# The first attention batch of a fused attention and MLP kernel: norms and Newton one slot sooner, its mix right behind the rank, landmark scaling on ACT, and 232 small unread products ahead of TensorE's queue

## The chip, the cores and the metric

The kernel runs on one core of a Trainium2 chip. The engines are named as the profile names them: PE (matrix products; PEld is its loading of weights), DVE (VectorE), ACT (ScalarE), POOL (GpSimd) and SP, whose queue issues most of the DMAs. The metric is the time of one execution on the device in microseconds; shorter is better.

## The reference

Three stages follow each other, in float32, for a batch of 8, with 576 tokens and a width of 512.

```python
# 1: Nystrom attention; 8 heads of 64, 32 landmarks (means over 18 tokens), scale 1/8
A, Bm, C = sm(q, k_lm), sm(q_lm, k_lm), sm(q_lm, k)
Z = Bm.T / (norm1(Bm) * norminf(Bm) + 1e-6)
for _ in range(6):
    Z = 2 * Z - Z @ Bm @ Z
x = A @ Z @ C @ v
# 2: a rank-32 mix over the tokens, then an MLP 512 -> 2048 -> 512
u = x + (x.T @ U @ V).T
x = u + relu(u @ w_ch1) @ w_ch2
# 3: a real 2-D Fourier mix, layer norm, a second MLP of the same size
u = x + real(fft2(x))
y = u + relu(layernorm(u) @ w_ch1) @ w_ch2
```

The MLP weights and U and V arrive as float64 words, and the kernel makes float32 of them on the chip.

## The kernel before

The MLPs are nearly all of the products. Each of their float32 products is made of three reduced ones (high by high, high by low, low by high), in chunks of 512 tokens, so that weights and activations have to be split into a high and a low part first: ACT copies the high part, DVE or POOL subtracts it.

The work runs in slots that are written out by hand. `Batch.steps` yields pairs of a slot number and a step for one batch of the attention, and the program runs them slot by slot; the order in which the steps are recorded is the order in which each engine takes its instructions, so an instruction that waits holds everything behind it on its engine. The steps of batch 0 begin at slot -21. From slot 0 the steps of a batch stand between pieces of the first MLP pass (`mlp.stream(0)`, whose products are L238 to L240 and L291 to L293). Batch 1 begins so early that its first steps lie among the last ones of batch 0. Ahead of the first MLP product PE thus has the whole of batch 0 and the first half of batch 1.

A batch goes as follows. `landmark` sums 18 tokens at a time on DVE (L726) and scales the sums into the tiles `kb` and `qb` (L728, on POOL), whose other places are zeroed once at the start. `kernel` multiplies `qb` and `kb` (L759, eight products, four column groups of 32 beside each other) and `kernel_norm` and `kernel_t` make Bm, its transpose and the sums behind its norms on DVE. `scores` is C (L823 and L828), with its maxima on DVE (L831) and its exponentials on ACT (L837 and L839). `norms` (L792), `residue` (L806) and six times `newton` (L969) make Z. `query` is A (L896, L903), `values` (L874) is C @ v, `mixed` (L951, L955) A @ U, `heads` (L984) and `rank` (L995) join them, and `mix` (L1011) writes two of the four blocks of u: ACT copies them out of PSUM (L1014), and they are split into the tiles `x` that the MLP reads (L50 and L51).

Two kinds of products fill slots: landmark sums of a later batch (`landmark_sums`, L738), and products of the identity matrix with itself that nobody reads (L1543). Beside this the weights of the first pass are converted on DVE, ACT and POOL (`convert`, L95 to L105, called by `direct`), from raw tiles that SP fetches (L87).

Of the kernel before, what the change touches and what calls it, by code (L numbers as in the profile page):

```python
# [9 lines left out]
F32 = mybir.dt.float32  # L10
# [12 lines left out]
LM, W = 32, 18  # L23
P = 128
# [11 lines left out]
def f32(ap):  # L36
    return ap.bitcast(F32)
# [3 lines left out]
def body(ctx: ExitStack, tc: tile.TileContext, qT, kT, vn, mU, mV, w11, w12, w21, w22,  # L41
         ident, bones, istack, tabs, out):
    nc = tc.nc
# [42 lines left out]
    def fetch_raw(raw, src):  # L86
        nc.sync.dma_start(raw, src.bitcast(U32))  # L87
# [82 lines left out]
    class Mlp:  # L170
# [17 lines left out]
        def fetch(self, nm, src):  # L188
            t = f32(self.weight(nm))
            if isinstance(src, tuple):  # L190
                for n, part in enumerate(src):
                    nc.sync.dma_start(t[:, :, 256 * n:256 * n + 256], part)
            else:
                nc.sync.dma_start(t, src)
# [461 lines left out]
    UB = 4  # L656

    def attention_constants(cp, t):
        t["ident"] = cp.tile([P, P], F32, name="ident_sb")
        nc.sync.dma_start(t["ident"], ident)  # L660
        t["U"] = cp.tile([P, 6, R], F32, name="U_sb")
        t["v"] = cp.tile([P, 5, DM], F32, name="v_")
        t["ETt"] = cp.tile([P, 2, P], F32, name="ETt")
        nc.gpsimd.memset(t["v"][64:P, 4, :], 0.0)
        nc.gpsimd.memset(t["ETt"][64:P], 0.0)
        for nm in ("kb", "qb"):
            t[nm] = cp.tile([P, 4, 64], F32, name=nm)
            nc.gpsimd.memset(t[nm], 0.0)
        for nm, src, n in (("bones", bones, P), ("istack", istack, R)):
            t[nm] = cp.tile([P, n], F32, name=nm + "_sb")  # L670
            nc.sync.dma_start(t[nm], src)
        t["at"] = cp.tile([P, 4, S], F32, name="at")
        t["W"] = cp.tile([P, 4, 64], F32, name="W")
# [22 lines left out]
    class Batch:  # L696
# [25 lines left out]
        def landmark(self, nm, g):  # L722

            src, dst = getattr(self, nm)[:, 2 * g:2 * g + 2, :], self.t[nm + "b"]
            s_ = self.pool.tile([P, 2, LM], F32, name="ls", bufs=2)
            nc.vector.tensor_reduce(s_, src.rearrange("p e (m w) -> p e m w", w=W), axis=AX.X, op=ALU.add)  # L726
            for j in range(2):
                nc.gpsimd.tensor_scalar_mul(dst[64 * j:64 * j + 64, 2 * g:2 * g + 2, 32 * (j ^ g):32 * (j ^ g) + 32],  # L728
                                            s_[64 * j:64 * j + 64], 1.0 / W if nm == "k" else 0.125 / W)

        def landmark_sums(self, nm, first, last):

# [55 lines left out]

        def norms(self):

            ps = self.bank("n" if self.b > 1 else "b")
            nc.tensor.matmul(ps[:, 0:P], self.t["bones"], self.dg.rearrange("p a b -> p (a b)"), start=True, stop=True)  # L792
            n = self.stat(4).rearrange("p (g k) -> p g k", k=2)
            nc.vector.tensor_reduce(n.rearrange("p g k -> p (g k)"), ps[:, 0:P].rearrange("p (a b) -> p a b", b=R),
                                    axis=AX.X, op=ALU.max)
            self.c = self.stat(2)
            nc.vector.tensor_tensor(self.c, n[:, :, 0], n[:, :, 1], op=ALU.mult)
            nc.vector.tensor_scalar_add(self.c, self.c, 1e-6)
            nc.vector.reciprocal(self.c, self.c)
# [221 lines left out]
        def steps(self, after):  # L1021

            H0, H1 = slice(0, 512), slice(512, 1152)
            a, b = (2, 1) if self.b > 1 else (0, 0)
            yield from ((2 * (nm == "q") + g - a, lambda nm=nm, g=g: self.landmark(nm, g)) for nm in "kq"
                        for g in (0, 1) if (self.b, nm) not in LANDMARKS)
            yield from ((5 - a, self.kernel), (6 - a, self.kernel_norm), (7 - a, self.kernel_t))
            if a:
                yield 6, self.norms
            yield 6, self.scores  # L1030
            if not a:
                yield 8, self.norms
            yield 9 - b, self.residue
            yield from ((10 - b + i, lambda i=i: self.newton(i)) for i in range(6))
            yield from ( (8, lambda: self.query(0)), (9, lambda: self.query(1)),
                        (9, lambda: self.query_exp(H0)), (9, self.scores_sum), (9, lambda: self.query(2)), (10, lambda: self.scores_t(0)),
                        (11, lambda: self.scores_t(1)), (11, self.scores_tail), (11, lambda: self.query_exp(H1)),
                        (11, lambda: self.query_norm(H0)), (12, self.values), (12, lambda: self.query_norm(H1)),
                        (13, lambda: self.query_t(0)), (13, self.query_tail), (14, lambda: self.query_t(1)),
                        (15, self.mixed), (16 - b, self.heads), (17 - b, self.rank))  # L1040
            if self.b:
                yield 13, lambda: self.mlp.get_tail(self.b)
                yield from ((15 + k // 2, lambda k=k: self.mlp.hand_tail(self.b, k)) for k in range(4))
            yield from ((19 + g, lambda g=g, n=n: self.mix(g, n)) for g in range(2) for n in range(2))
            if after:
                yield from ((r, lambda nm=nm: after.load(nm)) for r, nm in ((7, "k"), (10, "q"), (13, "v")))

# [269 lines left out]
    def pool(name, **k):  # L1317
        return tc.tile_pool(name=name, bufs=1, reuse_waits="tile", **k)
# [5 lines left out]
    def some(gen, n):  # L1324
        for _ in range(n):
            next(gen, 0)
# [156 lines left out]
    with pool("mm") as mp, pool("pm", space=PSUM) as pm:  # L1483
        mlp = Mlp(mp, pm, 3, passes)

        def direct():

            ws = [mlp.weight(nm) for nm in ("w1", "w2") for _ in range(HM)]
            raws = []
            seq = [*range(4), *range(HM, 2 * HM, 2), *range(4, HM), *range(HM + 1, 2 * HM, 2)]  # L1490

            def fetch():
                i = len(raws)
                if i < len(ws):
                    if i < EARLY:
                        raw = f32(mp.tile([P, 2, 512], F32R, name="g", bufs=HM)).rearrange(
                            "p a n -> p (a n)").bitcast(U32)
                    else:
                        raw = cv0.tile([P, 1024], U32, name="wraw", bufs=2)
                    fetch_raw(raw, srcs[0][seq[i]])  # L1500
                    raws.append(raw)

            for n in range(2):
                fetch()
                yield 1

            old = None
            for n, i in enumerate(seq):
                while len(raws) < min(max(n + 2, min(n + 3, EARLY)), len(ws)):
                    fetch()  # L1510
                new = convert(cv0, raws[n], ws[i], 2)
                for g in (new, old, old, new):
                    if g:
                        yield next(g)
                old = new
            yield from old

        EARLY = 8
        with pool("aa") as ap_, pool("ac") as ac, pool("cv0") as cv0, pool("pt", space=PSUM) as psb:
            t = {}  # L1520
            batches = [Batch(ap_, psb, t, b, mlp) for b in range(B)]
# [23 lines left out]
            with tc.manual_schedule():  # L1545
                for what in "kq":
                    batches[0].load(what)
                attention_constants(ac, t)
                small, large = attention_setup(t, ap_, cv0), direct()
                some(small, 1)  # L1550
                some(large, 1)
                batches[0].load("v")
                some(large, 1)
                convs = chained([small, large])
                for s in range(FIRST, 0):
                    slots.run(s)
                    if s - FIRST in (6, *range(10, 20)):
                        filler(s)
                    some(convs, 0 if s < FIRST + 4 else 1 + s % 2)
                later, gen = staging(cv0, 1, 2), mlp.stream(0)  # L1560
                for s in range(N + GAP - 8):
                    if s >= GAP or s in half:
                        next(gen)
                    else:
                        filler(s)
                    slots.run(s)
                    if s < GAP + 13:
                        some(convs, 2)
                        if s == GAP + 12:
                            some(convs, 99)  # L1570
                    else:
                        some(later, 1 if s % 3 == 2 else 2)
                some(later, 999)
                some(gen, 9)
# [120 lines left out]
```

## Time and profile before

| | |
|---|---|
| time, median of 3 runs | 1787.42 us (1785.45 to 1788.26) |
| the profiled execution, its own time | 1789.14 us |
| its span, first to last instruction | 1787.4 us |
| PE busy | 1757.6 us, 98% of the span |
| DVE, ACT, POOL busy | 1171.2, 735.6, 328.2 us |
| first MLP product starts | 57.95 us into the span |

The profiled execution took 1.74 us outside its span, and 1.72 us more than the median of the runs without a profile. All times of rows are in us from the start of the span. A PE busy for 98% says little by itself, since the profile counts a product that overlaps its neighbour as busy all along; what matters for a change at the begin of the program is when the first MLP product starts, and whether PE still waits for others after it.

### The profile page before, as it was taken

The page shows a single profiled execution, that of the slowest core. Times are in us where ns is not written, and L with a number is a line of the kernel's source. Part 1 is how long each engine was busy: PE and PEld are TensorE (multiplying, and loading weights), DVE is VectorE, ACT ScalarE, POOL GpSimd, SP SyncE. Part 2 cuts the span into 40 slices and gives each one's busy share as a digit, 9 for nine tenths or more (in the row PEclk, how much of TensorE's full clock was granted, in tenths as well). Part 3 has the DMA queues.
Part 4 walks back from the last instruction along what each step waited for, and adds up shares of the span by engine and source line. Part 5 has one row for each costly group of instructions (what it writes and reads, how often), then busy time and mean ns, then how long its engine had stood idle before and what let it go on. Part 6 is the DMA issues. An engine that isn't in the chain of part 4 may idle for free.

```text
span 1787.4 us, 30912 instructions
## 1 busy us (share of the span) xinstructions
PE 1757.6 (98%) x11905; PEld 1432.7 (80%) x11905; DVE 1171.2 (66%) x2028; ACT 735.6 (41%) x1520; POOL 328.2 (18%) x314
## 2 busy tenths in 40 slices
PE   6999999999999999999999999999999999999999
PEld 4777777777788888888878888888878888888887
DVE  7897666566322977888886665657575674577564
ACT  4554443444211333433342333434256445454642
POOL 3324211221110321211111122211111001100100
PEclk9999999999999999999999999999999999999999
DMA  7555456443536764546555954776688778878764
GB/s 254 182 174 171 152 175 206 155 162 105 179 137 249 242 234 154 183 164 216 179 179 193 329 200 148 273 281 201 222 290 273 216 243 257 261 228 247 223 214 153
DMA packets 215895, 371.00 MB, mean 208 GB/s; under 512 B 28970, under 2 KB 129930, under 8 KB 215748
## 3 DMA queue, kind: packets, MB, share of 16 engines
q1 hardware_dynamic: 211140, 359.59, 60.9%
q10 hardware_dynamic: 4608, 9.44, 1.4%
q8 instruction: 94, 1.54, 0.4%
q14 instruction: 53, 0.43, 0.1%
HBM read 262.18 MB, written 106.17 MB: 206 GB/s over the span
## 4 chain that ended last, share of the span: by engine, by line
PE 88%; DVE 7%; DMA 2%; ACT 1%; issue 1%; SPq 0%; POOL 0%; DVEq 0%; ACTq 0%
PE ps L291 9%; PE ps L293 9%; PE ps L292 9%; PE ps L238 9%; PE ps L240 8%; PE ps L239 8%; PE ps L329 7%; PE ps L331 7%; PE ps L330 7%; PE ps L554 1%; PE ps L553 1%; PE ps L555 1%; PE ps_f L77 1%; PE ps_f L76 1%; PE ps_f L75 1%
## 5 line engine op out<-in xcount | busy, mean ns | idle before, releaser
L238 PE MATMUL ps<-x,w 128*128 128x512 f32 x768 | 305.4, 398 | 0.2 <-DVE g L243 0.2
L291 PE MATMUL ps<-g,w 128*128 128x512 f32 x768 | 304.2, 396 | 0.0
L240 PE MATMUL ps<-x,w 128*128 128x512 f32 x768 | 299.8, 390 | 0.0
L293 PE MATMUL ps<-g,w 128*128 128x512 f32 x768 | 299.8, 390 | 0.0
L239 PE MATMUL ps<-x,w 128*128 128x512 f32 x768 | 299.4, 390 | 0.0
L292 PE MATMUL ps<-g,w 128*128 128x512 f32 x768 | 299.2, 390 | 0.0
L243 DVE SCALAR_TENSOR_TENSOR g<-ps,g 128x512 fp32r<-128x512 f32 x192 | 132.4, 690 | 206.7 <-ACT g L242 206.4
L242 ACT ACTIVATE g<-ps 128x512 fp32r<-128x512 f32 x192 | 114.0, 597 | 264.0 <-PE ps L240 263.4
L291 PEld LDWEIGHTS ps<-g,w 128*128 128x128 f32 x768 | 144.3, 188 | 31.9 <-issue 3.5
L240 PEld LDWEIGHTS ps<-x,w 128*128 128x128 f32 x768 | 144.1, 188 | 31.4
L293 PEld LDWEIGHTS ps<-g,w 128*128 128x128 f32 x768 | 144.1, 188 | 31.1
L238 PEld LDWEIGHTS ps<-x,w 128*128 128x128 f32 x768 | 144.3, 188 | 29.9 <-DVE g L243 0.6
L292 PEld LDWEIGHTS ps<-g,w 128*128 128x128 f32 x768 | 144.4, 188 | 27.4
L239 PEld LDWEIGHTS ps<-x,w 128*128 128x128 f32 x768 | 144.4, 188 | 26.9
L302 DVE TENSOR_TENSOR xf<-ps,xf 128x512 f32<-128x512 f32 x88 | 60.5, 687 | 86.7 <-PE ps L293 84.6
L406 ACT COPY ps<-ps 128x512 f32<-128x512 f32 x126 | 72.4, 575 | 94.4 <-PE ps L331 93.4
L51 POOL TENSOR_TENSOR stg<-cva,stg 128x512 fp32r<-128x512 f32 x48 | 65.4, 1363 | 216.8 <-ACT stg L50 190.4
L458 POOL TENSOR_TENSOR w<-w,w 128x512 f32<-128x512 f32 x24 | 33.3, 1389 | 362.1 <-DMA w<-rs 181.6
L329 PE MATMUL ps<-xs,w 128*128 128x512 f32 x240 | 94.2, 392 | 1.9 <-ACT ps L406 1.9
L331 PE MATMUL ps<-xs,w 128*128 128x512 f32 x240 | 94.1, 392 | 0.0
L330 PE MATMUL ps<-xs,w 128*128 128x512 f32 x240 | 93.9, 391 | 0.0
L51 POOL TENSOR_TENSOR x<-xf,x 128x512 fp32r<-128x512 f32 (+7 forms) x48 | 60.1, 1254 | 157.9 <-ACT x L50 122.7
(420 smaller groups left out, 3356.9 us busy)
## 6 DMA issues: line engine op xcount, KB each, us to landing
w<-e SPq DMA_DIRECT2D x84, 512.0 KB
w<-d SPq DMA_DIRECT2D x126, 256.0 KB
w<-d SPq DMA_DIRECT2D x60, 512.0 KB
wraw<-w SPq DMA_DIRECT2D x56, 512.0 KB
d<-stg SPq DMA_DIRECT2D x48, 512.0 KB
y<-xf SPq DMA_DIRECT2D x64, 256.0 KB
xf<-y SPq DMA_DIRECT2D x52, 256.0 KB
u<-u1T ACTq DMA_DIRECT2D x32, 288.0 KB
```

The lines of the kernel that those rows point to most:

```text
L51: (eng or nc.vector).tensor_tensor(lo, src, f32(hi), op=ALU.subtract)
L238: nc.tensor.matmul(ps, wh, xh, start=k == 0, stop=False)
L239: nc.tensor.matmul(ps, wl, xh, start=False, stop=False)
L240: nc.tensor.matmul(ps, wh, xl, start=False, stop=k == 3)
L242: nc.scalar.activation(g[:, 0, :], ps, AF.Relu)
L243: nc.vector.scalar_tensor_tensor(out=g[:, 1, :], in0=ps, scalar=0.0, in1=f32(g[:, 0, :]), op0=ALU.max, op1=ALU.subtract)
L291: nc.tensor.matmul(ps, wh, gh, start=k == m0, stop=False)
L292: nc.tensor.matmul(ps, wl, gh, start=False, stop=False)
L293: nc.tensor.matmul(ps, wh, gl, start=False, stop=k == m1 - 1)
L329: nc.tensor.matmul(ps, wh, xh, start=first and k == 0, stop=False, skip_group_check=True)
L330: nc.tensor.matmul(ps, wl, xh, start=False, stop=False, skip_group_check=True)
L331: nc.tensor.matmul(ps, wh, xl, start=False, stop=last and k == 1, skip_group_check=True)
```

## The change

Five edits, all of them about batch 0 and the begin of the program. (1) `attention_constants` zeroes `qb` and `kb` before the tiles `v` and `ETt`, and behind it 232 products of 32 by 32 columns of `qb` with itself go to PE; nothing reads them. (2) Batch 0 scales its landmark sums on ACT instead of POOL. (3) Its `kernel_t`, `norms`, `residue` and `newton` stand one slot sooner, hence `heads` and `rank` too, and `norms` takes its PSUM bank from "n" instead of "b". (4) All four calls of its `mix` move from slots 19 and 20 to slot 17, behind `rank`. (5) `direct` fetches one raw weight tile at its begin instead of two.

```diff
     def attention_constants(cp, t):
+        for nm in ("qb", "kb"):
+            t[nm] = cp.tile([P, 4, 64], F32, name=nm)
+            nc.gpsimd.memset(t[nm], 0.0)
         t["ident"] = cp.tile([P, P], F32, name="ident_sb")
...
         nc.gpsimd.memset(t["ETt"][64:P], 0.0)
-        for nm in ("kb", "qb"):
-            t[nm] = cp.tile([P, 4, 64], F32, name=nm)
-            nc.gpsimd.memset(t[nm], 0.0)
...
             for j in range(2):
-                nc.gpsimd.tensor_scalar_mul(dst[64 * j:64 * j + 64, 2 * g:2 * g + 2, 32 * (j ^ g):32 * (j ^ g) + 32],
-                                            s_[64 * j:64 * j + 64], 1.0 / W if nm == "k" else 0.125 / W)
+                (nc.gpsimd.tensor_scalar_mul if self.b else nc.scalar.mul)(
+                    dst[64 * j:64 * j + 64, 2 * g:2 * g + 2, 32 * (j ^ g):32 * (j ^ g) + 32],
+                    s_[64 * j:64 * j + 64], 1.0 / W if nm == "k" else 0.125 / W)
...
-            ps = self.bank("n" if self.b > 1 else "b")
+            ps = self.bank("b" if self.b == 1 else "n")
...
-            a, b = (2, 1) if self.b > 1 else (0, 0)
+            a, b = (2, 1) if self.b > 1 else (0, int(not self.b))
+            e = int(not self.b)
...
-            yield from ((5 - a, self.kernel), (6 - a, self.kernel_norm), (7 - a, self.kernel_t))
+            yield from ((5 - a, self.kernel), (6 - a, self.kernel_norm), (7 - a - e, self.kernel_t))
...
-                yield 8, self.norms
+                yield 8 - e, self.norms
             yield 9 - b, self.residue
...
-            yield from ((19 + g, lambda g=g, n=n: self.mix(g, n)) for g in range(2) for n in range(2))
+            yield from ((17 if e else 19 + g, lambda g=g, n=n: self.mix(g, n)) for g in range(2) for n in range(2))
...
-            for n in range(2):
-                fetch()
-                yield 1
+            fetch()
+            yield 1
...
-        EARLY = 8
+        EARLY, WARM = 8, 232
...
                 attention_constants(ac, t)
+                ps, warm = mlp.bank(), t["qb"].rearrange("p a m -> p (a m)")
+                for _ in range(WARM):
+                    nc.tensor.matmul(ps[0:32, 0:32], warm[:, 0:32], warm[:, 32:64], start=True, stop=True)
                 small, large = attention_setup(t, ap_, cv0), direct()
                 some(small, 1)
                 some(large, 1)
                 batches[0].load("v")
-                some(large, 1)
```

The first place is the begin of PE's queue. Before, the first product is that of `kernel`:

```order
L1688 UNCONDITIONAL_BRANCH
L759 MATMUL ps_b<-kb,qb 32x32 x8
L823 MATMUL ps_c<-k__226,qb 32x512 x8
L828 MATMUL ps_b<-k__226,qb 32x64 x4
L828 MATMUL ps_n<-k__226,qb 32x64 x4
L1543 MATMUL ps<-ident_sb 128x128 x6
L792 MATMUL ps_b<-dg,bones_sb 128x128
L896 MATMUL ps_c<-kb,q__229 32x64 x32
```

With the change (line numbers are some 1 to 3 higher here; L1552 is the line of the new products):

```order
L1691 UNCONDITIONAL_BRANCH
L1552 MATMUL ps<-qb 32x32 x232
L760 MATMUL ps_b<-kb,qb 32x32 x8
L824 MATMUL ps_c<-k__226,qb 32x512 x8
L829 MATMUL ps_b<-k__226,qb 32x64 x4
L829 MATMUL ps_n<-k__226,qb 32x64 x4
L1544 MATMUL ps<-ident_sb 128x128 x6
L793 MATMUL ps_n<-dg,bones_sb 128x128
L807 MATMUL ps_n<-BT 32x32 x8
L897 MATMUL ps_c<-kb,q__229 32x64 x32
L970 MATMUL ps_n<-ry 32x64 x8
L897 MATMUL ps_c<-kb,q__229 32x64 x32
```

The 232 products stand ahead of `kernel`, and the residue and the first Newton step come before the halves of `query` that they followed.

The second place is the begin of ACT's queue. Before:

```order
L46 ACT_TABLE_LOAD
L65 ACTIVATE wraw<-wraw 128x192
L767 ACTIVATE sB,st<-ps_b,st 128x32 x2
L837 ACTIVATE E,st<-ps_c,st 128x512
L839 ACTIVATE E,st<-ps_b,st 128x64
```

With the change:

```order
L46 ACT_TABLE_LOAD
L728 ACTIVATE kb<-ls 64x2x32 x4
L728 ACTIVATE qb<-ls 64x2x32 x4
L65 ACTIVATE wraw<-wraw 128x192
L768 ACTIVATE sB,st<-ps_b,st 128x32 x2
L838 ACTIVATE E,st<-ps_c,st 128x512
```

Eight scalings came in from POOL. Those that write `qb` write a tile that the 232 products read, so the first of them waits for the last of the 232.

The third place is PE around the mix of batch 0 (L1011, now L1012) and the scores of batch 1 (L823, now L824). Before:

```order
L995 MATMUL ps_n<-W,au 32x64 x8
L823 MATMUL ps_c<-k__372,qb 32x512 x8
L828 MATMUL ps_b<-k__372,qb 32x64 x4
L828 MATMUL ps_n<-k__372,qb 32x64 x4
L1543 MATMUL ps<-ident_sb 128x128 x12
L1011 MATMUL ps_n<-at,W 64x288 x4
L1011 MATMUL ps<-at,W 64x288 x4
L792 MATMUL ps_b<-dg,bones_sb 128x128
```

With the change:

```order
L985 MATMUL ps_n<-Y,ry 32x64 x8
L739 MATMUL ps<-k__609,ident_sb 128x128 x3
L996 MATMUL ps_n<-W,au 32x64 x8
L760 MATMUL ps_b<-kb,qb 32x32 x8
L1544 MATMUL ps<-ident_sb 128x128 x6
L1012 MATMUL ps_n<-at,W 64x288 x4
L1012 MATMUL ps<-at,W 64x288 x4
L824 MATMUL ps_c<-k__609,qb 32x512 x8
L829 MATMUL ps_b<-k__609,qb 32x64 x4
L829 MATMUL ps_n<-k__609,qb 32x64 x4
L1544 MATMUL ps<-ident_sb 128x128 x12
L793 MATMUL ps_b<-dg,bones_sb 128x128
```

All of the mix now lies ahead of the scores of batch 1, on ACT its copies ahead of their exponentials, and `heads` has one group of landmark sums (L739) less ahead of it.

## Rows read from the trace of the kernel before

**Rows 1.** The page: busy time and instructions; the chain that ended last, by engine.
```profile
PE 1757.6 (98%) x11905; PEld 1432.7 (80%) x11905; DVE 1171.2 (66%) x2028; ACT 735.6 (41%) x1520; POOL 328.2 (18%) x314
...
PE 88%; DVE 7%; DMA 2%; ACT 1%; issue 1%; SPq 0%; POOL 0%; DVEq 0%; ACTq 0%
```

**Rows 2.** Waits of PE, 0 to 58 us: total, times, longest.
```profile
PE ps_b L759 <- POOL qb L728: 10.5, 2, 9.4
PE ps_n L969 <- DVE cva L95: 3.8, 1, 3.8
```

**Rows 3.** Busy time by stretch: length, PE, PEld, DVE, ACT, POOL, clock, DMA.
```profile
58.00:80.00 22.00, 21.45 (x249) 16.78 (x247) 19.27 (x41) 13.27 (x31) 6.80 (x6) 1.00 0.72 235
80.00:140.00 60.00, 58.27 (x808) 43.69 (x809) 54.16 (x108) 32.71 (x82) 22.24 (x21) 1.00 0.49 160
```

**Rows 4.** Timeline of PE, 0 to 62 us, and one row at 82 us.
```profile
9.37 0.77 PE L759 MATMUL ps_b<-kb,qb 128*32 128x32 f32 x8 [9.37 <-POOL qb L728]
...
11.59 1.96 PE L823 MATMUL ps_c<-k__226,qb 64*32 64x512 f32 x16
...
13.69 2.35 PE L1543 MATMUL ps<-ident_sb 128*128 128x128 f32 x12
...
17.39 1.10 PE L896 MATMUL ps_c<-kb,q__229 128*32 128x64 f32 x64
...
24.33 1.11 PE L851 MATMUL ps_c<-ident_sb,E 128*128 128x128 f32 x4
...
44.73 1.09 PE L823 MATMUL ps_c<-k__372,qb 64*32 64x512 f32 x16
...
45.86 2.94 PE L1543 MATMUL ps<-ident_sb 128*128 128x128 f32 x24
...
57.95 0.50 PE L238 MATMUL ps<-x,w 128*128 128x512 f32 x1
...
61.26 0.65 PE L851 MATMUL ps_c<-ident_sb,E 128*128 128x128 f32 x4
...
81.89 0.46 PE L951 MATMUL ps_b<-U_sb,A 128*32 128x32 f32 x32
```

**Rows 5.** The chain of waits, 0 to 60 us: start, length, what.
```profile
1.64 5.75 DMA q__229<-qT
...
39.84 1.62 PE ps L738 x6
```

**Rows 6.** Timeline of POOL, 0 to 12 us: start, length, what.
```profile
0.73 0.52 POOL L664 MEMSET v__235<- 64x512 f32 x1 [0.29 <-POOLq L1684]
...
1.81 0.33 POOL L668 MEMSET qb<- 128x256 f32 x1
...
10.42 0.85 POOL L728 TENSOR_SCALAR qb<-ls 64x64 f32<-64x64 f32 x2 [0.65 <-DVE ls L726]
```

**Rows 7.** Timeline of DVE, 11.7 us.
```profile
11.72 0.23 DVE L765 TENSOR_REDUCE st<-ps_b 128x2 f32<-128x64 f32 x1
```

**Rows 8.** Busy time by stretch, columns as in rows 3.
```profile
11.70:58.00 46.30, 39.67 (x841) 30.49 (x841) 38.33 (x100) 24.65 (x72) 12.62 (x13) 0.93 0.68 232
```

**Rows 9.** The page, DMA queues: packets, MB, share.
```profile
q8 instruction: 94, 1.54, 0.4%
```

**Rows 10.** Timeline of PEld, 19.5 to 24 us.
```profile
19.54 0.30 PEld L903 LDWEIGHTS ps_b<-kb,q__229 128*32 128x32 f32 x16
23.72 0.44 PEld L969 LDWEIGHTS ps_n<-ry 32*32 32x32 f32 x16 [3.88 <-issue]
```

**Rows 11.** DMA queues, 20 to 23.7 us: packets, MB, share.
```profile
q1 hardware_dynamic: 354, 1.36, 98.2%
q8 instruction: 1, 0.02, 1.9%
```

**Rows 12.** Timeline of ACT, 41 to 51 us.
```profile
41.55 0.95 ACT L743 ACTIVATE kb<-ps 64x64 f32<-64x64 f32 x4 [0.48 <-PE ps L738]
...
48.83 0.69 ACT L837 ACTIVATE E<-ps_c,st 128x512 f32<-128x512 f32 x1 [3.44 <-PE ps L1543]
```

## The prediction

> **What bounds the kernel now.** I read the page first: the chain that ended last is 88% PE, 7% DVE [rows 1]. So PE's queue sets the time, and the question is when it starts on its main work and whether it waits afterwards. The list of PE's waits up to 58 us holds two that matter: 10.5 us for `qb`, nearly all of it ahead of the first product, and 3.8 us on the first Newton product [rows 2]. The busy time by stretch then shows that behind 58 us PE lacks only 22.00 - 21.45 = 0.55 us up to 80 us and 1.73 us in the next 60 [rows 3]. A shift of the first MLP product is therefore nearly a shift of the end: **the time moves as the first MLP product moves**. That product starts at 57.95 [rows 4]. What leads to it begins with the load of q until 7.39 and DVE's sums of it, then POOL's scalings until 10.42 + 0.85 = 11.27 [rows 5, 6], then `kernel`, whose sums DVE takes up at 11.72 [rows 7]. From there to 58 us DVE is busy for 38.33 of 46.30 us [rows 8]: PE sets the pace there, with DVE close behind, so a delay of DVE's reduction at 11.72 should reach 57.95 almost whole.
>
> **The 232 products.** They need only the zeroed `qb`, now POOL's first work, so they start at 0.73 + 0.33 = 1.1 us [rows 6]. Before, PE had nothing to do until 9.37 [rows 4], so up to there they are free. But they all go into the same 32 columns, so they run one behind the other, and the scalings into `qb` on ACT wait for the last.
>
> No row shows such a product alone, so its price has bounds. A float32 product of the identity with itself stands as two records, and 24 records in a row take 2.94 us [rows 4]: 122 ns for 128 columns, 31 for 32, 61 ns for a product of two. The early rows are slower: the eight score products take 1.96 us at 11.59 and 1.09 at 44.73, a factor of 1.8 [rows 4], which fits the lower of PE's two clock levels, 1.2 against 2.4 GHz, although the mean clock granted from 11.7 to 58 us is 0.93 [rows 8]. So a product costs 61 ns at the upper and 110 ns at the lower level, 232 of them 14.2 or 25.5 us, and the last ends at 15.3 or 26.6. I take a mixture. In before, the identity products at 13.69 (12 records in 2.35 us, 196 each) are still slow on the mean and `query` at 17.39 no longer is: the rise came 4.3 to 8.0 us behind the first product. If it does so again, 39 to 73 products run at 110 ns and the other 193 to 159 take 11.8 to 9.7 us: the end is 17.2 to 18.8, mean 18.0.
>
> **Their code.** PE's code comes by the instruction queue, 94 loads [rows 9] for 2 x 11905 records [rows 1], 253 in each. The 232 products are 928 records, 3.7 loads more, and they use them up in 17 us, where PE from 58 to 140 us takes 82 us for 2113 [rows 3]. The lower bound of a load is nothing. From 58 to 140 us there were 2113 / 253 = 8.4 loads with 2.28 us of idle PE in all [rows 3], at most 0.27 a load: 3.7 cost 1.0. The upper bound is the idle time of 3.88 us before 23.72, for which weight loading names no releaser [rows 10], while transfers filled 98.2% of the DMA engines and a single load of code came through [rows 11]: 3.7 x 3.88 = 14.4. I take 1.0, because the rows of 82 us hold many loads and the other one; the end is then 19.0. The Trainium skill (Runtime: NRT & Kernel Launch, section Instruction fetch mechanics) says that the sequencer fetches the next 16 KiB block while it executes the current one, and that crossing a boundary is "mostly hidden". By it the term would be 0 and the sum 1.0 smaller; the trace agrees from 58 us on (0.27 us a load) and seems to differ at 19.9 to 23.7 us.
>
> **From the last of them to DVE.** Four scalings on ACT follow: 0.95 us, as four of the same size take at 41.55 [rows 12]. From the end of POOL's scalings to DVE's reduction it was 11.72 - 11.27 = 0.45 [rows 6, 7]. So the reduction starts at 19.0 + 0.95 + 0.45 = 20.4 instead of 11.72: **+8.7**.
>
> **What is given back.** A PE kept busy should run `scores` at its later pace, 1.96 to 1.09 (-0.9); the two transposes of E at 24.33 may go from 1.11 to 0.65 [rows 4], -0.9 if both do, of which I take half, -0.45. The stall of 3.88 us should go too, since the code that PE lacked there is fetched during the 232 products. But DVE, which goes on through it, is idle in only 7.97 of the 46.30 us [rows 8]; I count that share, 0.17 x 3.88 = 0.7, of bounds 0 and 3.88. Together -2.0.
>
> **The slots.** `norms`, `residue` and Newton one slot sooner give a later step one group of landmark sums less ahead of it, 1.62 [rows 5], -1.6. The mix ahead of batch 1's `scores` costs PE nothing, the products are the same; but on ACT the exponentials of batch 1, which ran from 48.83 to 50.8 with PE's 2.94 us of identity products as their cover [rows 4, 12], now queue behind the mix's copies, and `norms` of batch 1 waits on them: +1.9 (bounds 0, if the cover holds, and 3.4, the wait ahead of them on ACT, if they come that much later). Sum +0.3. The other bank of `norms` and the raw tile fetched later cost nothing: batch 0's next user of bank "n" is `residue`, which waits for `norms` anyway, and the tile is read only after the conversions of the first one, which cover it; without that cover a conversion would wait for at most one transfer, the nearest being that of q, 5.75 us [rows 5], and I take 0.
>
> **The sum:** 8.7 - 2.0 + 0.3 = +7.0. The profiled execution took 1789.14, its span 1787.4; it would take 1796.1 with a span of 1794.4. The median is 1787.42, so the forecast for the median is **1794.4**.
>
> **The rivals.** *Code or clock lets the products run much longer.* All at the lower level they end at 26.6, and the reduction comes at 28.0: +16.3 - 2.0 + 0.3 gives about 1802; each load that stalls like the one of rows 10 adds up to 3.9. For it: the DMA engines are full while it happens [rows 11]. Against it: before, the pace rose by 17.39 with far fewer products. Chance 0.12.
>
> *The delay is lost in slack.* If the conversions of weights that DVE and ACT have yet to do fill the time in which they now wait, DVE's 7.97 us of idle time [rows 8] could take up nearly all of it: 1787, no change. Against it: the order in each queue is fixed, and the conversions stand behind the waiting reduction. Chance 0.12.
>
> *Faster: the products hide whole, and take the stall with them.* `mixed` runs 32 records of 32 columns in 0.46 us [rows 4], 14 ns each, 29 for a product, though in four column groups beside each other. At that price 232 end at 7.8, before q's sums do. It decides at (10.4 - 1.1) / 232 = 40 ns for a product: below it ACT waits for nobody. Then the scores (-0.9), both transposes (-0.9), the slot (-1.6), ACT's two last scalings in place of POOL's (0.48 for 0.85, -0.4) and, if PE is what counts, the whole stall (-3.9) stand against the +1.9 of the exponentials: -5.8, **1781.6**. Against it: they share one column group. The Trainium skill (TensorE: Matmul & The Clock Gate, section What's actually happening) calls the throttled clock the default that activity releases; this speaks for the purpose of such products, and the slow rows at 11.59 and 13.69 agree, but it doesn't shorten them. Chance 0.18. That the change doesn't do what it says can be left out: the products stand in PE's order.
>
> **The numbers.** Less than 0.2%, some 3.6 us, can't be told from no change here. The forecast, between +4 and +12 us by its bounds, has 0.58. Slower: 0.58 + 0.12 = 0.70; same 0.12; faster 0.18. The range leaves out most of the faster case and the longer half of the first rival: 1783 to 1803; the forecast's own is 1791 to 1800.
>
> **What would show it.** In the changed kernel's profile the 232 products end near 19 us; ACT's first scaling of `qb` waits for them; DVE reduces `kernel` near 20.4; code loads appear before 20 us; the stall ahead of the first Newton product is gone; the first MLP product starts near 65, and PE idles behind it as little as before. The prediction is wrong if the products end by 11 us, if the reduction is late but the MLP starts at 58 all the same, or if PE waits much longer or less behind its start.

## The result, and the profile after

The changed kernel takes 1801.5 us (median) against 1787.34 us for the one before in the same rounds: a ratio of 1.008, 95% interval 1.006 to 1.0101, so 10.7 to 18.0 us slower. One of the six executions took 2921.94 us at a granted clock of 0.556 and is not in the ratio; the median of the other five is 1799.94 us. A second measurement of the changed kernel further below gave 1800.5. The forecast of 1794.4 has the sign and its range holds the time, but the time moved by about twice the +7.0 that was forecast (by 12.6 us with the five, by 14.2 with all six). The profiled execution took 1803.06 us, with this page (the parts that answer to [rows 1, 9]):

```profile
span 1801.3 us, 31839 instructions
...
PE 1773.6 (98%) x12369; PEld 1449.6 (80%) x12369; DVE 1173.4 (65%) x2028; ACT 737.7 (41%) x1528; POOL 324.3 (18%) x306
...
q8 instruction: 97, 1.59, 0.4%
...
PE 84%; DVE 8%; DMA 4%; ACT 2%; issue 1%; SPq 0%; POOL 0%; ACTq 0%; DVEq 0%; POOLq 0%
```

PE has 464 records more, the 232 products at two each, and three loads of code more. The timeline of PE shows them and what they delay (it answers to [rows 4]):

```profile
1.10 9.14 PE L1552 MATMUL ps<-qb 128*32 128x32 f32 x223 [1.10 <-POOL qb L661]
11.60 4.21 PE L1552 MATMUL ps<-qb 128*32 128x32 f32 x128 [1.36 <-issue]
18.07 5.13 PE L1552 MATMUL ps<-qb 128*32 128x32 f32 x113 [2.26 <-issue]
23.64 0.45 PE L760 MATMUL ps_b<-kb,qb 128*32 128x32 f32 x8 [0.44 <-ACT qb L728]
...
24.56 1.09 PE L824 MATMUL ps_c<-k__226,qb 64*32 64x512 f32 x16
...
66.28 0.49 PE L793 MATMUL ps_b<-dg,bones_sb 128*128 128x128 f32 x2 [3.36 <-ACT E L840]
...
72.36 0.50 PE L238 MATMUL ps<-x,w 128*128 128x512 f32 x1
```

The products start at 1.10 as forecast and run in three pieces with two idle times between them, 1.36 and 2.26 us, for which the profile names no releaser ("issue"). They end at 23.2. `scores` now runs at its later pace (1.09 for 1.96), the stall ahead of the first Newton product is gone, and the first MLP product stands at 72.36 in place of 57.95: 14.4 us later.

The products don't keep one pace. By stretch (length, PE, PEld, clock, DMA; a record that lies across a boundary counts on both sides):

```profile
1.10:5.00 3.90, 3.90 (x73) 3.90 (x74) 1.00 0.80 278
5.00:10.24 5.24, 5.24 (x154) 5.16 (x153) 1.00 0.90 315
18.07:23.20 5.13, 5.13 (x113) 5.01 (x112) 0.67 0.02 4
```

At first a record takes 53 ns, later 34, and 45 in the last piece, where the granted clock is 0.67 on the mean: it fell after the two idle times. In the first stretch the column reads 1.00 at the slow pace too; the run with 32 products below shows that this is not to be taken for the upper level.

Of the 14.4 us, 13.0 are there already when DVE takes up `kernel` (timeline of ACT, then of DVE, against [rows 7]):

```profile
23.23 1.08 ACT L728 ACTIVATE qb<-ls 64x64 f32<-64x64 f32 x4 [15.30 <-PE ps L1552]
```

```profile
24.70 0.22 DVE L766 TENSOR_REDUCE st<-ps_b 128x2 f32<-128x64 f32 x1 [11.63 <-PE ps_b L760]
```

ACT had been idle for 15.3 us and DVE for 11.6. From this reduction to the first MLP product it takes 47.66 us, where it took 57.95 - 11.72 = 46.23: nothing is given back, 1.4 us are lost. Besides the 3.36 us above, one more long wait on this way is new:

```profile
29.86 0.33 PE L807 MATMUL ps_n<-BT 32*32 32x32 f32 x16 [2.10 <-DVE st L795]
```

The residue (L807) now follows `norms` directly and waits 2.10 us for DVE's part of the norms. Before, the first half of `query` stood between the two, and PE had no such wait.

### The profile page after: what moved, and what is told of

It reads as the page before. It is cut to its first block, busy times and chain, and to the rows that moved or that the text cites. A ratio compares the mean times of both kernels' runs of the same rounds, so it can differ in the third digit from the quotient of the medians.

```text
span 1801.3 us, 31839 instructions
## 1 busy us (share of the span) xinstructions
PE 1773.6 (98%) x12369; PEld 1449.6 (80%) x12369; DVE 1173.4 (65%) x2028; ACT 737.7 (41%) x1528; POOL 324.3 (18%) x306
## 4 chain that ended last, share of the span: by engine, by line
PE 84%; DVE 8%; DMA 4%; ACT 2%; issue 1%; SPq 0%; POOL 0%; ACTq 0%; DVEq 0%; POOLq 0%
PE ps L291 9%; PE ps L293 8%; PE ps L292 8%; PE ps L238 8%; PE ps L240 8%; PE ps L239 8%; PE ps L329 7%; PE ps L330 7%; PE ps L331 7%; PE ps L554 1%; PE ps L553 1%; PE ps L555 1%; PE ps_f L77 1%; PE ps_f L76 1%; PE ps_f L75 1%
```

## The experiments

The first four take the products and the other edits apart. Theories on record: the products alone are late and carry the delay to the end (1); a good part comes from the other edits (2); only the columns that pass through TensorE count, not the code (3). Times are medians beside the kernel before of the same rounds.

**The changed kernel without the products.**

```diff
-                ps, warm = mlp.bank(), t["qb"].rearrange("p a m -> p (a m)")
-                for _ in range(WARM):
-                    nc.tensor.matmul(ps[0:32, 0:32], warm[:, 0:32], warm[:, 32:64], start=True, stop=True)
```

> The changed kernel without the 232 products, all other edits kept. Theory 1 (the products alone are late: their own pace and two waits for code of 3.6 us together put off DVE's reduction of kernel by 13.0 us, and that delay reaches the end): DVE's reduction near 11.3 us, the wait of about 3.9 us for code is back ahead of an early Newton step, the first MLP product at 57 to 59 us, time 1786 to 1790 us. Theory 2 (a good part of the 14 us comes from the other edits, above all batch 1's exponentials behind the mix's copies, where PE waited 3.36 us): first MLP product at 61 us or later, time 1791 us or more.

1795.48 against 1787.36, ratio 1.004 (1.0028 to 1.0052). DVE's reduction stands at 11.83, the wait for code is back, and yet the first MLP product comes at 62.32. Theory 1 fails in its "alone": the other edits make the kernel slower by themselves. Waits of PE in this kernel up to 75 us:

```profile
PE ps_b L760 <- ACT qb L728: 10.4, 2, 9.3
PE ps_c L897 <- issue: 3.5, 1, 3.5
PE ps_b L793 <- ACT E L840: 3.2, 1, 3.2
```

The wait of 3.2 us for batch 1's exponentials is there without the products too.

**The products alone, in the kernel before.**

```diff
     def attention_constants(cp, t):
+        for nm in ("qb", "kb"):
+            t[nm] = cp.tile([P, 4, 64], F32, name=nm)
+            nc.gpsimd.memset(t[nm], 0.0)
...
-        for nm in ("kb", "qb"):
-            t[nm] = cp.tile([P, 4, 64], F32, name=nm)
-            nc.gpsimd.memset(t[nm], 0.0)
...
-        EARLY = 8
+        EARLY, WARM = 8, 232
...
+                ps, warm = mlp.bank(), t["qb"].rearrange("p a m -> p (a m)")
+                for _ in range(WARM):
+                    nc.tensor.matmul(ps[0:32, 0:32], warm[:, 0:32], warm[:, 32:64], start=True, stop=True)
```

> The kernel before with the 232 products ahead of PE's queue (qb and kb zeroed first), nothing else of the change. Theory 1: products end near 23 us as in the changed kernel, two POOL scalings follow, reduction near 24.5 us, no wait for code at the first Newton step, first MLP product at 69 to 72 us, time 1798 to 1803 us. Theory 2: the products cost less than the whole, 1794 to 1797 us.

1802.46, ratio 1.0085 (1.0071 to 1.0098): as slow as the whole change. So the parts don't add up: +8.1 without the products, +15.1 with them alone, +14.2 with all. In its profile the products end at 20.2 with waits of 0.60 and 1.44 us:

```profile
1.10 9.08 PE L1551 MATMUL ps<-qb 128*32 128x32 f32 x223 [1.10 <-POOL qb L661]
10.78 4.21 PE L1551 MATMUL ps<-qb 128*32 128x32 f32 x128 [0.60 <-issue]
16.43 3.74 PE L1551 MATMUL ps<-qb 128*32 128x32 f32 x113 [1.44 <-issue]
...
67.64 0.50 PE L238 MATMUL ps<-x,w 128*128 128x512 f32 x1
```

DVE's reduction stands at 22.32; from there to the first MLP product it is 45.32, 0.9 us less than before. That is the whole give-back of a stall of 3.88 us that no longer appears and of faster scores.

**As many columns in a quarter of the records.** 58 products of 128 columns.

```diff
-        EARLY, WARM = 8, 232
+        EARLY, WARM = 8, 58
...
-                    nc.tensor.matmul(ps[0:32, 0:32], warm[:, 0:32], warm[:, 32:64], start=True, stop=True)
+                    nc.tensor.matmul(ps[0:32, 0:128], warm[:, 0:32], warm[:, 64:192], start=True, stop=True)
```

> The changed kernel with 58 products of 128 columns in place of 232 of 32: as many columns through TensorE, a quarter of the records (232 of code in place of 928). Theory 1: no wait for code inside them, end at 17 to 20 us in place of 23.2, reduction near 19 to 21.5, time 1795 to 1798 us. Theory 3 (the code waits only take the place of a slower pace, columns alone count): end at 23 us, time 1800 to 1803 us.

1794.86, ratio 1.004 (1.0028 to 1.0052). One piece, no wait in it:

```profile
1.10 14.77 PE L1552 MATMUL ps<-qb 128*32 128x128 f32 x116 [1.10 <-POOL qb L661]
```

It ends at 15.9, sooner than theory 1 said. Its 127 ns a record are a mean: 19 records lie in the first 3.9 us, 205 ns each, and 99 in the 10.87 us behind, 110 each (PE, PEld, clock, DMA; the column reads 1.00 in both):

```profile
1.10:5.00 3.90, 3.90 (x19) 3.25 (x20) 1.00 0.80 268
5.00:15.87 10.87, 10.87 (x99) 10.60 (x97) 1.00 0.92 308
```

Theory 3 falls: with the same columns, a quarter of the records saves 6.6 us of time. A wait without a releaser does come, but later, after 349 records of products, near the 223 + 128 of the changed kernel:

```profile
28.09 0.31 PE L904 MATMUL ps_b<-kb,q__229 128*32 128x64 f32 x5 [2.51 <-issue]
```

**As many records in four column groups.**

```diff
-                for _ in range(WARM):
-                    nc.tensor.matmul(ps[0:32, 0:32], warm[:, 0:32], warm[:, 32:64], start=True, stop=True)
+                for i in range(WARM):
+                    j = 32 * (i % 4)
+                    nc.tensor.matmul(ps[j:j + 32, 0:32], warm[:, 0:32], warm[:, 32:64], start=True, stop=True, skip_group_check=True)
```

> The changed kernel with its 232 products dealt out over the four column groups in turn: as many records, but four products beside each other. Theory 1 with code as a limit of its own: pace alone would let them end near 8 us, but the records that are there at the start run out after some 110 products and three loads must come, so they end at 13 to 19 us, most of it waiting for code; reduction 1 to 1.5 us behind that, time 1789 to 1797 us. Theory 3 (pace alone counts): they end at 8 to 9 us, no one waits for them, reduction near 11.3 us, time 1784 to 1789 us.

1799.04, ratio 1.0069 (1.0054 to 1.0083), a little above the range of theory 1 and far from theory 3. The timeline of PE:

```profile
1.10 3.21 PE L1553 MATMUL ps<-qb 128*32 128x32 f32 x223 [1.10 <-POOL qb L661]
9.05 1.93 PE L1553 MATMUL ps<-qb 128*32 128x32 f32 x128 [4.74 <-issue]
12.79 1.72 PE L1553 MATMUL ps<-qb 128*32 128x32 f32 x113 [1.80 <-issue]
14.98 0.51 PE L760 MATMUL ps_b<-kb,qb 128*32 128x32 f32 x8 [0.47 <-ACT qb L728]
15.71 0.33 PE L760 MATMUL ps_b<-kb,qb 128*32 128x32 f32 x7 [0.22 <-ACT qb L728]
19.07 0.26 PE L760 MATMUL ps_b<-kb,qb 128*32 128x32 f32 x1 [3.03 <-issue]
```

The pieces break off after the same 223 and 128 records as with one column group, at whatever time that is, and a third time 128 records later (113 + 8 + 7), inside `kernel`. That shows a limit of its own that goes by the count of instructions: here 223 records are done at 4.31 us and PE stands still until 9.05. Transfers fill the DMA engines meanwhile, and one load of code comes through (DMA queues, 4.3 to 9.1 us, against [rows 11]):

```profile
q1 hardware_dynamic: 1232, 1.80, 102.3%
q8 instruction: 1, 0.02, 1.2%
```

In the changed kernel's own two waits it is otherwise: the transfers take less than half of the DMA engines, and no load of code falls into them (10.2 to 11.6 and 15.8 to 18.1 us):

```profile
q1 hardware_dynamic: 100, 0.10, 30.8%
q1 hardware_dynamic: 211, 0.37, 44.5%
```

What the waits have in common is the time between a load of code and PE's going on, 2.2 to 2.7 us in each of these (the tenth of a us in which the load's packet shows in the queue of code, q8, and the first record behind the wait):

| | load of code, us | PE goes on, us |
|---|---|---|
| kernel before | 21.1 | 23.72 |
| changed kernel | 9.1, 15.7 | 11.60, 18.07 |
| products alone | 8.3, 14.2 | 10.78, 16.43 |
| wide products | 25.5 | 28.09 |
| four column groups | 6.5, 10.1, 16.7 | 9.05, 12.79, 19.07 |

So full DMA engines are not needed for such a wait. What puts a load at its time was not tried.

The second four ask what the other edits cost, and whether products that hide altogether help. Theory 4: the mix was PE's work while batch 1's exponentials ran. Theory 5: the sooner norms and Newton, the scalings or the raw tile cost it.

**The mix back in slots 19 and 20, with the products** (all else as changed).

```diff
-            yield from ((17 if e else 19 + g, lambda g=g, n=n: self.mix(g, n)) for g in range(2) for n in range(2))
+            yield from ((19 + g, lambda g=g, n=n: self.mix(g, n)) for g in range(2) for n in range(2))
```

> The changed kernel, products included, with batch 0's mix back in slots 19 and 20. Theory 4 (formed from the first runs: the mix was what PE did while batch 1's exponentials ran, and ahead of the scores it leaves PE waiting 3.2 us for them): no wait above 1.5 us ahead of batch 1's norms product, first MLP product 2 to 4 us sooner after DVE's first reduction than the 47.7 us of the changed kernel, time 1796 to 1800 us. Theory 5 (norms and Newton a slot sooner, the ACT scalings or the raw tile are what costs): the interval stays 47 to 48 us, time 1800 to 1803 us.

1800.72 against 1788.17, ratio 1.0066 (1.0052 to 1.008). The wait ahead of batch 1's norms is gone, but the first MLP product follows the reduction (20.57) by 47.27 us, as good as the 47.66 of the changed kernel. Behind late products the mix matters little.

**The same without the products.** The edits of the first and the fifth run together.

> The changed kernel without the 232 products and with batch 0's mix back in slots 19 and 20; left of the change are norms and Newton a slot sooner, the scalings on ACT and the one raw tile. Theory 4: first MLP product at 57 to 60 us in place of 62.3, 1786 to 1791 us. Theory 5: at 61 to 63 us, 1792 to 1796 us.

1789.76, ratio 1.0007 (0.9999 to 1.0016), no more to be told from before. Against 1795.48 with the mix in slot 17, without the products the mix costs several us. The mark of the first MLP product, at 62.20, says otherwise and misleads: its span is only 0.9 us longer than before.

**The mix alone, in the kernel before.**

```diff
-            yield from ((19 + g, lambda g=g, n=n: self.mix(g, n)) for g in range(2) for n in range(2))
+            yield from ((19 + g if self.b else 17, lambda g=g, n=n: self.mix(g, n)) for g in range(2) for n in range(2))
```

> The kernel before with batch 0's mix moved to slot 17, behind rank, and nothing else of the change. Theory 4: PE waits about 3 us ahead of batch 1's norms product, first MLP product at 60 to 62 us, time 1789 to 1793 us. Theory 5: 57.5 to 58.5 us, 1786 to 1788.5 us.

1792.01, ratio 1.0024 (1.0015 to 1.0032): theory 4 holds. PE waits 3.31 us for the exponentials in this profile. How that comes about is read from DVE's timeline, here of the changed kernel:

```profile
58.89 1.29 DVE L51 TENSOR_TENSOR x<-u1T,x 128x512 fp32r<-128x512 f32 x2 [1.08 <-ACT x L50]
61.32 1.47 DVE L51 TENSOR_TENSOR x<-u1T,x 128x512 fp32r<-128x512 f32 x2 [1.14 <-ACT x L50]
...
63.31 1.28 DVE L832 TENSOR_REDUCE st<-ps_c 128x1 f32<-128x512 f32 x2
```

and from ACT's:

```profile
61.45 0.62 ACT L50 CAST x<-u1T 128x512 fp32r<-128x512 f32 x1 [0.15 <-ACT x L50]
65.15 0.69 ACT L838 ACTIVATE E<-ps_c,st 128x512 f32<-128x512 f32 x1 [3.08 <-DVE st L835]
```

In the kernel before, DVE took the maxima of batch 1's scores ahead of the splits of the mix:

```profile
46.99 1.29 DVE L831 TENSOR_REDUCE st<-ps_c 128x1 f32<-128x512 f32 x2
...
53.91 1.29 DVE L51 TENSOR_TENSOR x<-u1T,x 128x512 fp32r<-128x512 f32 x2 [2.31 <-ACT x L50]
```

Now the splits stand ahead, wait twice for ACT, and hold up the maxima; ACT then has nothing to do for 3.08 us. It isn't ACT's queue that is full. In the profile of the mix alone DVE's order is the same, and the wait has a second price: behind it the granted clock is 0.52 for 7 us, where the kernel before has 1.00 from 48 to 58 us (PE, PEld, DVE, ACT, POOL, clock, DMA):

```profile
56.00:63.00 7.00, 5.79 (x94) 5.14 (x94) 6.72 (x14) 3.33 (x11) 2.54 (x2) 0.52 0.42 169
```

**32 products alone, in the kernel before**, few enough to end at 4.7 us. Against the products alone, above:

```diff
-        EARLY, WARM = 8, 232
+        EARLY, WARM = 8, 32
```

> The kernel before with 32 of the products alone: they end by 5 us, long before the scalings, and their 128 records let PE ask for its first load of code sooner. If the wait of 3.9 us for code sets the pace: it is gone, and the first MLP product comes at 54 to 55 us, time 1783 to 1785 us. If DVE sets the pace there (theory 1's reading of the give-back): the wait is gone or short, the first MLP product at 56.5 to 58 us, time 1785.5 to 1788 us. If code comes when it will: the wait stays, at another place, 1786 to 1789 us.

1789.31, ratio 1.0014 (1.0005 to 1.0023). The stall of 3.9 us ahead of the first Newton product is gone, and nobody waits for the products; the time is no better, if anything a little worse. The first MLP product stands at 56.41, 1.5 us sooner, but PE has new waits ahead of it:

```profile
PE ps_b L936 <- DVE A L922: 1.5, 1, 1.5
...
PE ps L738 <- DMA k__405<-kT: 1.3, 1, 1.3
```

So the gain of 1.5 us is lost again further on; the offset of the MLP's products against before goes from -1.4 near 700 us to +0.2 at the end. Nor did these products keep the clock up. PE is idle from 4.72 to 9.49, the clock is 0.50 behind that, and the scores take 1.96 us as in the kernel before, where the column reads 1.00 (first this run, then before):

```profile
9.00:14.60 5.60, 3.76 (x51) 1.95 (x52) 4.34 (x12) 1.03 (x5) 2.23 (x5) 0.50 0.81 256
11.75 1.96 PE L823 MATMUL ps_c<-k__226,qb 64*32 64x512 f32 x16
...
9.00:15.00 6.00, 4.32 (x54) 2.51 (x55) 4.87 (x14) 1.03 (x5) 2.06 (x5) 1.00 0.83 267
```

So a 1.00 of this column at the begin can't be taken for the level. Products that hide and end just ahead of `kernel`, with the clock still up, were not run.

The last four look at the rest.

**Wide products and the mix back in slots 19 and 20.** The edits of the third and fifth run together.

> The changed kernel with 58 products of 128 columns in place of the 232, and batch 0's mix back in slots 19 and 20. With the wide products no wait for code falls inside them, so that the mix can be seen behind a late start (the wide products alone gave 1794.9 us). If the mix costs its 3 to 6 us behind a late reduction too: 1789 to 1792 us, no wait of 3 us ahead of batch 1's norms product. If a late start leaves something else last, so that the move of the mix is then free: 1793 to 1796 us.

1793.15 against 1788.77, ratio 1.0026 (1.0017 to 1.0034), between the two cases; the interval overlaps that of the wide products with the mix in slot 17. Reduction to first MLP product: 63.42 - 17.75 = 45.67, against 65.28 - 17.37 = 47.91. What the mix costs behind a late reduction stays open between 0 and some 3 us.

**The scalings on ACT alone.**

```diff
-                nc.gpsimd.tensor_scalar_mul(dst[64 * j:64 * j + 64, 2 * g:2 * g + 2, 32 * (j ^ g):32 * (j ^ g) + 32],
-                                            s_[64 * j:64 * j + 64], 1.0 / W if nm == "k" else 0.125 / W)
+                (nc.gpsimd.tensor_scalar_mul if self.b else nc.scalar.mul)(
+                    dst[64 * j:64 * j + 64, 2 * g:2 * g + 2, 32 * (j ^ g):32 * (j ^ g) + 32],
+                    s_[64 * j:64 * j + 64], 1.0 / W if nm == "k" else 0.125 / W)
```

> The kernel before with batch 0's landmark scalings on ACT and nothing else. The last two take 0.5 us in place of POOL's 0.85: 0 to 0.5 us faster, 1786 to 1788.5 us. If they hold up what ACT has for the weights' conversions: 1788.5 to 1790 us.

1787.08, ratio 0.9993 (0.9985 to 1.0002): no change that can be told.

**Norms and Newton a slot sooner, alone.**

```diff
-            ps = self.bank("n" if self.b > 1 else "b")
+            ps = self.bank("b" if self.b == 1 else "n")
...
-            a, b = (2, 1) if self.b > 1 else (0, 0)
+            a, b = (2, 1) if self.b > 1 else (0, int(not self.b))
+            e = int(not self.b)
...
-            yield from ((5 - a, self.kernel), (6 - a, self.kernel_norm), (7 - a, self.kernel_t))
+            yield from ((5 - a, self.kernel), (6 - a, self.kernel_norm), (7 - a - e, self.kernel_t))
...
-                yield 8, self.norms
+                yield 8 - e, self.norms
```

> The kernel before with batch 0's norms, residue and Newton a slot sooner (and norms in the other bank) and nothing else. By the prediction's slot term alone 1.6 us sooner, 1785 to 1787 us. If DVE sets the pace, so that steps taken sooner put off the softmax work of query behind them: 1788 to 1791 us, with a wait of PE for DVE at the second half of A's transpose.

1791.12, ratio 1.0014 (1.0005 to 1.0022): not 1.6 us sooner, but some 2 later. A reason stands in DVE's list of waits, 10 to 60 us:

```profile
DVE sm L908 <- PE ps_c L896: 3.4, 1, 3.4
DVE x L51 <- ACT x L50: 3.1, 1, 3.1
```

The wait for code still comes at the same place in PE's queue, by the count of instructions, but that place is now the last record of `query`'s second half (L896, 3.5 us) and not a Newton product. DVE has nothing else to do there and waits 3.4 us; in the kernel before it worked through the stall. This profile also has a granted clock of 0.57 from 36 to 40 and from 53 to 57 us, where that of the kernel before has 1.00; how much of the 2 us is the clock and how much DVE's wait was not tried.

**The changed kernel once more.**

> The changed kernel once more, on the chip of these runs. If the waits for code inside the 232 products vary from one execution to the next: 1798 to 1803 us with a spread of several us between runs, and in this profile other lengths of these waits than 1.36 and 2.26 us. If they are fixed by the place of the code: the same two waits within 0.2 us, and 1801 to 1802 us.

1800.5, ratio 1.0069 (1.0055 to 1.0083). The waits vary:

```profile
1.10 8.77 PE L1552 MATMUL ps<-qb 128*32 128x32 f32 x223 [1.10 <-POOL qb L661]
10.77 8.01 PE L1552 MATMUL ps<-qb 128*32 128x32 f32 x241 [0.90 <-issue]
...
68.87 0.50 PE L238 MATMUL ps<-x,w 128*128 128x512 f32 x1
```

One wait of 0.90 us in place of 1.36 and 2.26, the products end at 18.8, and DVE's reduction stands at 20.28.

## Why the sign was right and the size half

**The products' pace** was right: 223 records in 9.14 us and 128 in 4.21 are 82 and 66 ns a product, between the forecast's 110 and 61, and the mixture is there as well: some 107 ns a product in the first 3.90 us (73 records), 66 later. Without waits they would end near 18.2 us (1.10 + 9.14 + 241 records at the later pace, 8.0), forecast 18.0.

**Their code** was mis-sized for the first profile and right for the second: 1.0 forecast, waits of 3.62 and of 0.90 measured. After the longer waits the last 113 records also took 5.13 us where the pace of the piece before gives 3.7, at a granted clock of 0.67, a price that the forecast had no term for. Together that is 4.0 of the 4.3 us by which the delay of the reduction exceeds the forecast in the first profile. The form of the term was wrong: it is no price per load, but a stock of records at the start, 128 more with each load, and a wait where the next load is late. The four column groups show it: PE stands still 4.74 us where the profile names nothing else that holds it. Their three waits, 3.2 us on the mean, lie near the 3.88 of [rows 10, 11]; those behind one column group lie between that and 0.27. That full DMA engines hold the loads up, as the forecast's upper bound had it, doesn't fit the changed kernel's own waits (30.8% and 44.5%), and what does hold them up stays open.

**From the products to DVE** 0.95 + 0.45 = 1.4 was forecast, and 24.70 - 23.20 = 1.5 came. The delay of the reduction, +8.7 forecast, is +13.0 in the first and +8.6 in the second profile.

**What is given back, -2.0, and the slots, +0.3, are the steps that failed.** In the second profile, where the delay is as forecast, the first MLP product is 10.9 us late and not 7.0. The scores and transposes did get faster and the stall did go, as written, but the products alone bring back only 0.9 us, and 32 hidden ones nothing in the time: that DVE, busy for 38 of 46 us there, takes over as the bound fits this, as does PE's wait for it in the run with 32, but was not tested by itself. The run with 32 also can't show what a clock kept up is worth, since its clock had fallen again. In the slots both terms were wrong, each measured alone: -1.6 for the sooner norms and Newton came out as +2.4 (interval 0.9 to 3.9), and its trace shows the stall on products that DVE waits for, but a lower clock in two places too; +1.9 for the mix came out as +3.8 (2.7 to 5.7), and not by ACT's copies but by DVE's splits ahead of the maxima, with the lower clock behind the wait as a part of it that was not taken apart. In the changed kernel the first of these can't act, since its stall is gone; in its place stands the wait of 2.10 us ahead of the residue, which the slot term left out. There 3.36 us of waiting for the exponentials stand in the profile, and yet moving the mix back changed the time by 0.8 us only (1800.72 against 1801.5), which can't be told from nothing.

**"The time moves as the first MLP product moves"** holds for the changed kernel (+14.4, and +13.9 in the span) but is loose by up to some 3 us in the others: +6.3 and +3.0 for the mix alone, +4.3 and +0.9 without products and with the mix back. Most of the difference arises between some 1314 and 1329 us: with products matched by their number, the lag against the kernel before changes there by -2.6 to +0.3 us from one profile to the next. For 1.6 us of this the profiles show the reason: the granted clock of the kernel before falls there, and at the same products it doesn't in the changed kernel, where it is 1.00 from 1330 to 1345 us (PE, clock, DMA; kernel before, then four column groups):

```profile
1322.00:1326.00 4.00, 4.00 (x13) 0.57 1.07 384
1336.00:1342.00 6.00, 5.39 (x17) 0.72 1.05 383
```

The two profiles whose lag does not shrink there, those of 32 products and of four column groups, have the fall too. So a lag against this one profile can end 1.6 us smaller without any edit doing it, and the good agreement for the changed kernel is in part luck: its lag is 16.5 us near 1310 and 13.9 behind 1329. What makes the clock fall there was not tried. Nor is it settled why the products alone were measured at +15.1 by the median with a profile at +10.8: their runs went from 1798.3 to 1806.0, and only the profiled one shows its waits.

**The rivals.** The faster one fails at its own point of decision: 66 to 82 ns a product against 40. Nor was that point enough: in four column groups 223 records in 3.21 us are 29 ns a product, and the waits for code still make them late. Where the products do hide, in the run with 32, the stall goes, but the 3.9 us counted for it become 1.5 at the first MLP product and nothing in the time. The one with longer code waits has part of the truth, in size though not in the 26.6 us: 1801.5 lies outside the forecast's own 1791 to 1800 and near that rival's 1802. That the wide range holds it is owed to the room left for that rival; in the forecast's own sum the delay was too small for the first profile, and the give-back did not come in either. The delay was not lost in DVE's idle time.

## What to carry to other kernels

Work that fills an idle engine is free only until the first instruction that others wait for: compute its end from rows, and count its instructions as well as its columns, since here 58 wide products cost 6.6 us less than 232 narrow ones with the same columns. When a step is moved, look at what the other engines have ahead of their next instruction at that place, on DVE above all: a stall that an engine worked through can become one that it waits out. Look at the granted clock behind each new wait, too: here 7 us at 0.52 followed on the wait that the mix brought. And a mark such as the first product of the main loop is worth checking against the end of the span before it is taken for the time.

## What was not expected of the hardware

TensorE's supply of instructions was a limit of its own at the program's begin: the unread products stopped after 223 of their matrix product records, near 10 us with one column group and at 4.31 us with four, and went on only after idle times of 0.6 to 4.74 us that differ between executions of the same program (3.62 and 0.90 us in all for the changed kernel). PE went on 2.2 to 2.7 us behind a load of code, whether transfers filled the DMA engines or not. And the products' pace changed at the begin although the column of the granted clock reads 1.00 throughout: records of 128 columns took some 205 ns in the first 3.9 us and 110 behind, on the mean, those of 32 columns 53 and then 34.
